# GFNet filter beside a GELU layer on one core: inverse along m2 with a stationary table, DMA transposes, new load order

## The chip, the cores and the metric

One core of a Trainium2 chip. TensorE (PE) multiplies into PSUM, VectorE (DVE), ScalarE (ACT) and GpSimd (POOL) work on SBUF (the first two also read PSUM), SyncE (SP) issues transfers. The metric is device time in microseconds (us); lower is better.

## The reference

```python
xn = layernorm(x)                      # x: 2048 tokens x 640, bf16, no scale or shift
X  = rfft2(xn); X = X * (w_r + 1j*w_i) # over tokens and width: 2048 x 321
A  = irfft2(X)                         # back to 2048 x 640
B  = gelu(xn @ w1 + b1) @ w2 + b2      # 640 -> 1536 -> 640, tanh GELU
out = x + A + B
```

## The kernel before

The 2048 tokens are 128 partitions times 16 chunks c (token 16p + c); a chunk is 128 tokens by 640.

*Planner.* Every piece of work is an `op` with candidate engines, a priority and the buffers it reads and writes. `schedule` (L201) simulates the engines with costs per operation (`mm_us`, `dve_us`, `act_us`) and takes, engine by engine, the ready op of highest priority (`PRIO`, L115); an op with two candidates goes to the engine that ends it first. SP's ops keep the written order. `sync` turns the order into semaphore waits. PSUM is eight banks, handed out by `Pool` within zones (`ZONE`, L114). So the written code gives dependences, and the planner the order on each engine.

*Stages.*
1. Loads (L494 to L530), all from SP: x in eight pieces of two chunks into XV, W1 in three pieces, the tables, the filter w in 18 pieces into Wf, and more tables.
2. Normalisation per two chunks (L543 to L559): `bn_stats` and `bn_aggr` on VectorE, a power on GpSimd, then a scale and shift (L569). The result is transposed on TensorE (L576, five 128x128 pieces) and copied to xnT. VectorE folds it twice (L588, L592; sums and differences of mirrored halves), TensorE multiplies by G (DFT over the 128 partitions, L596) and the result goes to XW.
3. Layer 1 (L606 to L618): four blocks of 512 tokens; for each of 12 feature chunks five passes of 512 columns and one GELU on ScalarE into gT.
4. Spectral stage, eight pairs (L639 to L713): a width group with table E (`five`, L621: 8 passes with 128 rows, 8 with 32 rows in quarter tiles), copied to Xb; the transform along the 16 remaining tokens with mtab in 64x64 tiles (L652), copied to Y; the filter on VectorE (L671, L676) into Z; four small copies of the remaining columns to Zs (L686 to L692); the inverse along m2 (L696): Z is the stationary operand, the 128-column table ntab the moving one, 20 passes of 128 columns a pair, so the result comes out with the width on the partitions; copied to XV (L710).
5. Width back, eight groups of two chunks with table GE (L728), copied to Wf and unfolded by VectorE (L736, L741).
6. Layer 2 per chunk (L753): 24 passes of 320 columns; two more with H (L758) add the spectral part into the same PSUM; x, loaded again (L748), has b2 added on GpSimd (L749); VectorE adds both into ost (L761), which is stored.

W2 lies in XW's space, so its load waits for all width groups of stage 4 (L716). Nearly all TensorE work has line L467 (`mms`) in the profile, nearly all copies L474 (ScalarE) or L477; they are told apart by the names of tiles.

```python
load(W2, w2v, B_w2b, F * D * 2, after=pb_ops)                       # L716
lst.append((ps(dps.slot, 128 * g, 128 * g + 128), z(r, k0, 128), rh, n == 0, n == 1))   # L705
```

Of the kernel before, what the change touches and what calls it, by code (L numbers as in the profile page):

```python
# [12 lines left out]
S = 2048  # L13
# [14 lines left out]
def _tables():  # L28

# [8 lines left out]
    for s2 in range(16):  # L38
        for m1 in range(64):
            qq, lo, pair, hi = m1 // 32, m1 // 16 % 2, m1 % 16 // 2, m1 % 2  # L40
            ang = 2 * pi * ((m1 * (16 * s1 + s2)) % 2048) / 2048
            g, h = (2 * pair + qq) * 8 + hi * 4 + lo, (2 * pair + hi) * 8 + qq * 4 + lo
# [13 lines left out]
    M = np.zeros((128, 2, 2, 2, 64))  # L56
    N = np.zeros((2, 2, 128, 128))
    for sp in range(2):
        for hi in range(2):
            for lo in range(2):  # L60
                for m2 in range(16):
                    s2 = np.arange(16)
                    a1 = 2 * pi * ((m2 * s2) % 16) / 16
                    c, s = np.cos(a1), np.sin(a1)
                    a2 = 2 * pi * ((s2 * (2 * m2 + 1)) % 32) / 32
                    c2, t2 = np.cos(a2), np.sin(a2)
                    r, u = hi * 64 + s2 * 4 + lo, hi * 64 + s2 * 4 + 2 + lo
                    p = lo * 16 + m2
                    zero = sp and hi == 0 and lo == 0
                    pq = 32 + lo * 16 + (m2 if zero else 15 - m2)  # L70
                    (rr, ir), (ri, ii) = M[:, sp, 0].transpose(1, 0, 2), M[:, sp, 1].transpose(1, 0, 2)
                    if zero:
                        rr[r, p], ri[r, p], ir[r, p], ii[r, p] = c, s, -s, c
                        rr[u, pq], ri[u, pq], ir[u, pq], ii[u, pq] = c2, t2, -t2, c2
                    else:
                        rr[r, p], rr[u, p], ir[r, p], ir[u, p] = c, s, -s, c
                        ri[r, p], ri[u, p], ii[r, p], ii[u, p] = s, -c, c, s
                        rr[r, pq], rr[u, pq], ir[r, pq], ir[u, pq] = c, s, s, -c
                        ri[r, pq], ri[u, pq], ii[r, pq], ii[u, pq] = -s, c, c, s
                    if hi:  # L80
                        continue
                    for qq in range(2):
                        r, u = s2 * 8 + qq * 4 + lo, s2 * 8 + qq * 4 + 2 + lo
                        P, Q = 64 * qq + p, 64 * qq + pq
                        NA, NB = N[sp]
                        if sp and lo == 0 and qq == 0:
                            NA[P, r], NB[P, r], NA[Q, u], NB[Q, u] = c, s, c2, t2
                            continue
                        Q = 64 * qq + 32 + lo * 16 + 15 - m2
                        NA[P, r], NA[Q, r], NB[P, r], NB[Q, r] = c, c, s, -s  # L90
                        NA[P, u], NA[Q, u], NB[P, u], NB[Q, u] = -s, -s, c, -c
    T["M"] = M
    T["N"] = np.stack([N[:, 0], N[:, 1], -N[:, 1]], axis=1).transpose(2, 0, 1, 3)
# [3 lines left out]

def mm_us(n):
    return max(n / 2400.0 + 0.003, 0.0265)
# [6 lines left out]
def act_us(n, ptr=0):  # L106
    return 0.052 + n / 1200.0 + 0.092 * ptr
# [23 lines left out]
class Pool:  # L131

# [7 lines left out]
    def find(self, buf, now):  # L140

        size, n = buf.size, len(self.free)
        lo, hi = buf.zone or (0, n)
        best = None
        for i in range(lo, hi - size + 1, size):
            if any(self.busy[i:i + size]):
                continue
            t = max(self.free[i:i + size])
            key = (max(t, now), sum(not b for b in self.busy[i & ~1:(i & ~1) + 2]), sum(not b for b in self.busy[i & ~3:(i & ~3) + 4]), t)
            if best is None or key < best[0]:  # L150
                best = (key, t, i)
        return best and best[1:]
# [18 lines left out]
BIAS = {"dve": 0.0}  # L171
LAT = {"pe": 0.2, "dve": 0.12, "act": 0.15, "pool": 0.1}


class Sched:

# [8 lines left out]
    def op(self, engs, prio, emit, reads=(), writes=(), after=(), nbytes=0, gate=(), rate=330e3, bias=BIAS):  # L185
# [4 lines left out]
        o.nbytes, o.rate, o.bias = nbytes, rate, bias  # L190
# [9 lines left out]

    def schedule(self):  # L201
        free = {e: 0.0 for e in self.engines}
        dma_free = 0.0
        pend = {e: [] for e in self.engines}
# [12 lines left out]
        def avail(o):  # L217
            o.ready = max([0.0] + [d.end for d in o.deps] + [d.start for d in o.gate])
            for e, _ in o.engs:
                pend[e].append(o)  # L220
# [4 lines left out]
        while left:  # L225
            best = None
            for e in self.engines:
                cands = []
                for o in pend[e]:
# [64 lines left out]
    def sync(self):  # L294


        allops = sorted(self.ops, key=lambda o: o.start)
        place = {o: (e, i) for e in self.engines for i, o in enumerate(self.order[e])}
        for o in self.ops:
            need = []  # L300
            for d in set(o.deps):
                if d.nbytes == 0 and d.eng == o.eng:
                    if o.eng == "pe":
                        continue
                need.append(d)
            o.waits = need

# [40 lines left out]
    def emit(self, es, last):  # L348
# [30 lines left out]
        block.tensor(run("pe"))  # L379


def bass_parallel_sum__spectral_gfnet__dense_activation_gelu__prompt_kernel(
# [21 lines left out]
    with ExitStack() as es:  # L404
# [23 lines left out]
        W1 = sb("W1", [128, 5, F])  # L428
        gT = sb("gT", [128, NFC, S])
        xnT = sb("xnT", [128, 5, S])  # L430
        XV = sb("XV", [128, 16 * D])
        XW2 = sb("XW2", [128, 16 * D])
        Wf = sb("Wf", [128, 32 * KP])
        xb4 = sb("Xb", [128, 2, 4 * KP])
        Yb = sb("Y", [128, 2, 4 * KP])
        TT = sb("T", [128, 11 * D])
        Zb = sb("Z", [128, 2, 4 * KP])
        Zs = sb("Zs", [128, 2, 2, 256])
        ost = sb("ost", [128, 3, D])
        xrt = sb("xr", [128, 4, D])  # L440
        xot = sb("xo", [128, 3, D], F32)
        PS = [es.enter_context(nc.psum_tensor(f"ps{i}", [128, 1024], F32)) for i in range(4)]

        XN, X1, XF = 0, 4 * D, 7 * D
        V = view(XV, 0, [[2048, 5], [128, 16], [1, 128]])
        Xa = view(XW2, 0, [[2048, 5], [128, 16], [1, 128]])
        W2 = view(XW2, 0, [[D, NFC], [1, D]])
        YO, Y2, YF = 0, 6 * D, 10 * D

        def ps(slot, lo, hi):  # L450
            return PS[slot // 2][:, (slot % 2) * 512 + lo:(slot % 2) * 512 + hi]

        def ps2(slot, n):
            return PS[slot // 2][:, :].rearrange("p (b n) -> p b n", b=2)[:, :, 0:n]

        psum = Pool(8)
        SMALL = [("dve", 0.066 + 128 / 960), ("pool", 0.35), ("act", act_us(128))]
        p_xn, p_x1, p_xf, p_xb, p_y, p_t, p_z, p_zs = Pool(4), Pool(3), Pool(4), Pool(2), Pool(2), Pool(2), Pool(2), Pool(2)
        p_yo, p_y2, p_yf, p_xr, p_xo, p_os = Pool(3), Pool(2), Pool(3), Pool(4), Pool(3), Pool(3)

        def load(dst, src, buf, nbytes, after=(), reads=(), rate=330e3):
            return K.op([("sp", 0.45)], 0, lambda e, _: e.dma_start(dst, src), reads=reads, writes=[buf], after=after, nbytes=nbytes, rate=rate)  # L462

        def mms(lst):
            def f(e, _):
                for o_, lw, rh, st, sp_ in lst():
                    ins = e.matmul(o_, lhsT=lw, rhs=rh, start=st, stop=sp_)  # L467
                return ins
            return f

# [9 lines left out]

        B_mh, B_xbpad, B_wpad = Buf("mhalf"), Buf("xbpad"), Buf("wpad")
# [315 lines left out]
```

## Time and profile before

| | |
|---|---|
| median of 3 runs (lowest, highest) | 176.54 us (176.17, 176.83) |
| profiled execution: span from first to last instruction (its whole time is not printed) | 175.1 us |
| TensorE busy | 154.2 us (88%) |
| VectorE / ScalarE / GpSimd busy | 109.6 / 82.1 / 32.5 us |
| moved by DMA | 16.64 MB |

Busy time is the union of an engine's instructions, and a pass's end is modelled, so a TensorE row's duration is longer than the step to the next pass. In a timeline row the first number is the start in us from the span's start, the second the time that the merged group covers, and xN the number of instructions in it. Some pass records are missing from the trace, a few per cent.

### The profile page before, as it was taken

Reading aid. Unit: us, or ns where it says so; the run is one execution under the profiler, and the core shown is the slowest. Engines: PE = TensorE matmul, PEld = TensorE weight load, DVE = VectorE, ACT = ScalarE, POOL = GpSimd, SP = SyncE. Lnnn points to the kernel's source line nnn. Section 1 sums busy time; section 2 is a strip of 40 time slices with the busy share of each in tenths; the row PEclk is TensorE's granted clock in tenths of the full one; section 3 lists DMA queues with packets and bytes.
Section 4 is the critical chain, followed back from the end, with each engine's and each line's share of the span. In section 5 each row is a group of like instructions: output and inputs, shape, how many; then the busy total and the mean of one; then the engine's idle time right before and its main releaser. Section 6 shows DMA issues by size and latency. Waiting matters only on the chain.

```text
span 175.1 us, 3375 instructions
## 1 busy us (share of the span) xinstructions
PE 154.2 (88%) x1350; PEld 95.2 (54%) x1361; DVE 109.6 (63%) x296; ACT 82.1 (47%) x129; POOL 32.5 (19%) x42
## 2 busy tenths in 40 slices
PE   0046999999999997887899999999999999998992
PEld 0034455455555454454557667777777775554771
DVE  1789959999993496999913988383745641001211
ACT  2023776668797999999875321011010104543000
POOL 1110110110110011011190033334353333000300
PEclk9999999999999999999999999999999999999999
DMA  5999999999900000005932022222232211000121
GB/s 147 304 374 384 139 103 94 100 113 102 237 16 2 4 0 4 0 4 152 373 116 75 0 79 75 75 79 75 75 113 75 78 39 37 4 0 0 37 78 40
DMA packets 14856, 16.64 MB, mean 95 GB/s; under 512 B 1272, under 2 KB 13560, under 8 KB 14840
## 3 DMA queue, kind: packets, MB, share of 16 engines
q1 hardware_dynamic: 14840, 16.42, 42.8%
q8 instruction: 11, 0.18, 0.5%
q14 instruction: 5, 0.04, 0.1%
HBM read 13.79 MB, written 2.62 MB: 94 GB/s over the span
## 4 chain that ended last, share of the span: by engine, by line
PE 77%; ACT 12%; DMA 4%; DVE 3%; issue 1%; SPq 1%
PE ps L467 74%; DMA b1t<-in_B_b_dram 4%; ACT Xb L474 3%; ACT XV L474 3%; PE ps L576 3%; ACT Y L474 3%; ACT gT L616 1%; SPq L462 1%; ACT L616 1%; DVE T L592 1%; DVE T L569 1%; ACT Zs L474 1%; DVE T L588 1%; DVE ost L761 0%; DVE stats L550 0%
## 5 line engine op out<-in xcount | busy, mean ns | idle before, releaser
L467 PE MATMUL ps<-xnT,W 128*128 128x512 bf16 x229 | 57.3, 387 | 1.9 <-ACT xnT L474 0.8
L467 PE MATMUL ps<-XW,gT 128*128 128x320 bf16 x384 | 55.4, 299 | 0.8 <-ACT gT L616 0.8
L467 PEld LDWEIGHTS ps<-XW,gT 128*128 128x128 bf16 x384 | 37.2, 98 | 16.1 <-ACT gT L616 1.9
L616 ACT ACTIVATE gT<-ps,b1col 128x512 bf16<-128x512 f32 x48 | 32.8, 686 | 19.3 <-PE ps L467 19.2
L761 DVE TENSOR_TENSOR ost<-ps,xo 128x640 bf16<-128x640 f32 x16 | 13.2, 824 | 40.4 <-PE ps L467 40.4
L467 PEld LDWEIGHTS ps<-xnT,W 128*128 128x128 bf16 x240 | 22.1, 99 | 24.3 <-ACT gT L616 2.6
L749 POOL TENSOR_TENSOR xo<-xr,b2bc 128x640 f32<-128x640 bf16 x16 | 22.4, 1405 | 53.3 <-DVE ost L761 53.1
L474 ACT ACTIVATE Wf<-ps 128x640 bf16<-128x640 f32 x8 | 5.6, 704 | 37.3 <-PE ps L467 37.3
L550 DVE BATCH_NORM_STATS2 stats<-XV 128x6 f32<-128x320 bf16 x32 | 13.9, 467 | 4.4 <-DMA XV<-in_A_x_dram 4.4
L671 DVE TENSOR_TENSOR T<-Y,Wf 128x1288 bf16<-128x1288 bf16 x16 | 12.5, 823 | 2.4 <-ACT Y L474 2.3
L554 POOL TENSOR_TENSOR rstd<-ve,mhalf 128x2 f32<-128x2 f32 x8 | 5.7, 707 | 42.9 <-DVE ve L553 42.9
L474 ACT ACTIVATE XV<-ps 128x640 bf16<-128x640 f32 x16 | 11.1, 707 | 2.5 <-PE ps L467 2.5
L467 PE MATMUL ps<-ntab,Z 128*128 128x128 bf16 x128 | 9.8, 220 | 1.8 <-ACT Y L474 1.8
L474 ACT ACTIVATE XW<-ps 128x640 bf16<-128x640 f32 x13 | 9.1, 702 | 4.7 <-PE ps L467 4.4
L592 DVE TENSOR_TENSOR T<-T 128x256 bf16<-128x256 bf16 x64 | 11.2, 233 | 0.0
L474 ACT ACTIVATE xnT<-ps 128x640 bf16<-128x640 bf16 x8 | 5.6, 701 | 11.5 <-PE ps L576 11.5
L474 ACT ACTIVATE Y<-ps 128x644 bf16<-128x644 f32 x16 | 10.9, 706 | 0.1
L477 DVE CAST Wf<-ps 128x640 bf16<-128x640 f32 x8 | 6.6, 823 | 6.8 <-PE ps L467 6.4
L736 DVE TENSOR_TENSOR Wf<-Wf 128x640 bf16<-128x640 bf16 x16 | 10.1, 673 | 0.4
L467 PEld LDWEIGHTS ps<-ntab,Z 128*128 128x128 bf16 x128 | 7.6, 98 | 4.9 <-ACT Y L474 2.6
L477 POOL COPY Zs<-Z 128x128 bf16<-128x128 bf16 x9 | 3.4, 383 | 34.5 <-DVE Z L676 34.5
L477 DVE CAST Xb<-ps 128x640 bf16<-128x640 f32 x8 | 7.1, 883 | 4.3 <-PE ps L467 4.3
(41 smaller groups left out, 139.7 us busy)
## 6 DMA issues: line engine op xcount, KB each, us to landing
XV<-in_A_x_dram SPq DMA_DIRECT2D x8, 320.0 KB, 7.9
xr<-in_A_x_dram SPq DMA_DIRECT2D x16, 160.0 KB, 2.2
out_dram<-ost SPq DMA_DIRECT2D x16, 160.0 KB, 1.8
W<-in_B_w_dram SPq DMA_DIRECT2D x3, 640.0 KB, 9.2
XW<-in_B_w_dram SPq DMA_DIRECT2D x1, 1920.0 KB, 8.4
Wf<-in_A_w_r_dram SPq DMA_DIRECT2D x7, 160.5 KB, 16.2
Wf<-in_A_w_i_dram SPq DMA_DIRECT2D x7, 160.5 KB, 15.9
gtab<-c_G SPq DMA_DIRECT2D x1, 512.0 KB, 7.4
```

The lines of the kernel that those rows point to most:

```text
L467: ins = e.matmul(o_, lhsT=lw, rhs=rh, start=st, stop=sp_)
L474: return e.activation(dst(), src(), ACT.Copy, scale=scale)
L477: return e.tensor_copy(dst(), src())
L550: K.op([("dve", 0.4)], pr, lambda e, _, c=c, h=h: e.bn_stats(stats[:, c, 6 * h:6 * h + 6], view(XV, c * D + H2 * h, [[1, H2]])), reads=[B_ ...
L554: K.op([("pool", 0.6)], pr, lambda e, _, a=a, b=b: e.tensor_tensor(out=rstd[:, a:b], in0=ve[:, a:b], in1=mhalf[:, a:b], op=ALU.pow), reads ...
L576: ins = e.transpose(ps(tps.slot, 0, 512).bitcast(BF)[:, 128 * j:128 * j + 128], xnv(128 * j, [[1, 128]]), ident[:])
L592: K.op([("dve", dve_us(2 * n, 2))], pr - 0.2, lambda e, _, op=op, x1v=x1v, xfv=xfv, o_=o_, o0=o0, o1=o1, n=n: e.tensor_tensor(out=xfv(o_, ...
L616: K.op([("act", act_us(512, 1))], pr + PRIO["gelu"], lambda e, _, q4=q4, fc=fc, hps=hps: e.activation(gT[:, fc, 512 * q4:512 * q4 + 512], ...
L671: t_ops[pair].append(K.op([("dve", dve_us(4 * KP, 2))], pr, lambda e, _, k=k, Y=Y, TB=TB, pair=pair: e.tensor_tensor(out=view(TT, TB.slot ...
L736: K.op([("dve", dve_us(D, 2))], pr + 2, lambda e, _, k=k, op=op, yo=yo, y2=y2: e.tensor_tensor(out=view(Wf, Y2 + y2.slot * 2 * D + (H2 - 1 ...
L749: K.op([("pool", pool_us(640))], 50, lambda e, _, xr=xr, xo=xo: e.tensor_tensor(out=xot[:, xo.slot, :], in0=xrt[:, xr.slot, :], in1=b2bc[: ...
L761: K.op([("dve", dve_us(640))], 95, lambda e, _, xo=xo, os_=os_, fps=fps: e.tensor_tensor(out=ost[:, os_.slot, :].rearrange("p (h n) -> p h ...
```

## The change

- *Inverse.* ntab shrinks to 64x64 tables and becomes the stationary operand; Z is the moving one, 320 columns, in four 64x64 tiles; Zs and its copies are gone. The result has its tokens on the partitions, is copied in two instructions to a buffer U (in gtab's space or behind T), and a DMA transpose per q, issued from SP, puts it into XV with the width on the partitions. The H table and the layout of the filter rows (every fourth partition) change with it.
- *x* has its own buffer X for the whole kernel and is not loaded again; XV now holds what XW held and then the transposed result. W2 has its own buffer and is loaded before the spectral stage. The final sums and stores use W1's space once layer 1 is done.
- *Loads* in order of first use: x alone for chunks 0 and 1, then in pairs; the first third of W1 from ScalarE's queue.
- *Layer 1* in blocks of 1, 1, 2, 2, 2, 4, 4 chunks. Thirty passes on a zeroed tile stand first on TensorE.
- *Width groups* of 2, 3, 3, 3, 3, 2 chunks, all full-height passes first, then the quarter-height ones. Folds take two chunks in one instruction.
- *Layer 2*: chunks 0 to 3 (`KEEP`) are done before the last stage, their sum kept in xnT's space; the 640 columns are split 512 + 128; the last chunk ends in two halves.
- *Planner*: a cost for a change of tile shape, `HOLD` to stay in a shape, other latencies and zones.

```diff
+BLOCKS = [(0, 1), (1, 1), (2, 2), (4, 2), (6, 2), (8, 4), (12, 4)]
+GROUPS = [(0, 2), (2, 3), (5, 3), (8, 3), (11, 3), (14, 2)]
+BYDMA = ()
+KEEP = (0, 1, 2, 3)
...
+        B_wps = Buf("warmps", psum)
+        pe([("128", 30 * 0.108)], 300, lambda: [(psb(B_wps.slot, [[1, 128]]), warm[:], warm[:], True, True) for _ in range(30)],
+           reads=[B_warm], writes=[B_wps])
...
+        load_x(0, 1)
+        load_w1(0, "act")
         load(ident[:], const["I"], B_id, 32768)
+        load_x(1, 1)
         load(b1t[:], b1v, B_b1, 3072)
+        load_w1(1)
+        load_x(2, 2)
+        load_w1(2)
+        load(gtab[:], const["G"], B_g, 524288)
+        for c in range(4, 16, 2):
+            load_x(c, 2)
...
+            for v in range(2):
+                dps = Buf(f"dps{pair}_{v}", psum, 2, ZONE["dps"])
+                d_ops.append(pe([("64", 2 * mm_us(H2) + 0.02)], PRIO["ipc"] - pair / 5 + 0.02 * (1 - v), lambda pair=pair, v=v, Z=Z, dps=dps: [
+                    (psb(dps.slot + qq, [[1, H2]], 0, 64 * hi, 64),
+                     part(ntab, 64 * qq, 64, (1 if pair == qq == hi == 0 else 0) * 192 + 64 * ((0, 2), (1, 0))[v][r], [[1, 64]]),
+                     part(Zb, 64 * qq, 64, Z.slot * 4 * KP + (2 * hi + r) * KP + v, [[1, 2], [2, Q4]]), r == 0, r == 1)
+                    for r in range(2) for qq in range(2) for hi in range(2)], reads=[Z, B_n], writes=[dps]))
...
+                def evac(e, name, U=U, v=v, uv=uv, dps=dps):
+                    for o_, w in ((0, 128), (512, 32)):
+                        ins = copy(lambda: uv(U, o_ + 2 * w * v, [[D, 2], [w, 2], [1, w]]), lambda: psb(dps.slot, [[512, 2], [Q4, 2], [1, w]], o_ // 4))(e, name)
+                    return ins
...
+            for qq in range(2):
+                q = 2 * pair + qq
+                K.op([("sp", 1.6)], 0, lambda e, _, q=q, qq=qq, U=U, uv=uv: e.dma_start_transpose(
+                    XV[:, :, 128 * q:128 * q + 128], uv(U, D * qq, [[1, D]])), reads=[U, B_u], writes=[B_v[q]], nbytes=163840, rate=150e3)
...
+                if kept:
+                    kps = Buf(f"kps{c}", psum, 2, ZONE["fps"])
+                    second(c, kps, 0, D, pr, [kept_ops[-2]] if len(kept_ops) > 1 else [pb_ops[-2]])
+                    xo2 = Buf(f"kx{c}")
+                    kept_ops.append(K.op([("dve", dve_us(D))], 30, lambda e, _, kps=kps, xov=xov, shaped=shaped: e.tensor_tensor(
+                        out=xov(0, D), in0=shaped(psb(kps.slot, [[1, D]])), in1=xov(0, D), op=ALU.add), reads=[kps, xo], writes=[xo2]))
```

## Rows read from the trace of the kernel before

**Rows 1.** Page, its head and part 1: busy time, share of the span, instructions.

```profile
span 175.1 us, 3375 instructions
...
PE 154.2 (88%) x1350; PEld 95.2 (54%) x1361; DVE 109.6 (63%) x296; ACT 82.1 (47%) x129; POOL 32.5 (19%) x42
```

**Rows 2.** Timeline, first 17 us: start, duration, engine, line, operation [idle before].

```profile
3.76 1.28 DVE L550 BATCH_NORM_STATS2 stats<-XV 128x6 f32<-128x320 bf16 x3 [3.76 <-DMA XV<-in_A_x_dram]
...
7.24 0.72 POOL L554 TENSOR_TENSOR rstd<-ve,mhalf 128x2 f32<-128x2 f32 x1 [6.15 <-DVE ve L553]
...
9.61 0.80 DVE L569 TENSOR_SCALAR T<-XV,rstd,nmr 128x640 bf16<-128x640 bf16 x2
...
10.11 1.25 PE L576 MATMUL ps<-ident,T 128*128 128x128 bf16 x10 [0.81 <-DVE T L569]
...
10.86 0.49 DVE L477 COPY xnT<-ps 128x640 bf16<-128x640 bf16 x1
...
15.72 0.70 ACT L474 ACTIVATE xnT<-ps 128x640 bf16<-128x640 bf16 x1 [1.04 <-PE ps L576]
...
16.48 1.46 PE L467 MATMUL ps<-xnT,W 128*128 128x512 bf16 x3 [0.80 <-ACT xnT L474]
...
19.23 1.28 ACT L616 ACT_TABLE_LOAD   x1
```

**Rows 3.** Timeline of TensorE: layer-1 passes early and later.

```profile
18.27 2.20 PE L467 MATMUL ps<-xnT,W 128*128 128x512 bf16 x5
...
24.08 1.24 PE L467 MATMUL ps<-xnT,W 128*128 128x512 bf16 x5
```

**Rows 4.** Timeline of TensorE near the end, and VectorE's last addition.

```profile
168.30 3.42 PE L467 MATMUL ps<-XW,gT 128*128 128x320 bf16 x24
...
171.56 0.43 PE L467 MATMUL ps<-Wf,htab 128*128 128x320 bf16 x2
172.03 0.82 DVE L761 TENSOR_TENSOR ost<-ps,xo 128x640 bf16<-128x640 f32 x1 [2.71 <-PE ps L467]
```

**Rows 5.** Timeline, spectral stage between the width passes.

```profile
64.47 0.73 ACT L474 ACTIVATE XV<-ps 128x640 bf16<-128x640 f32 x1
...
67.10 1.08 PE L467 MATMUL ps<-etab,XW 128*128 128x160 bf16 x16
...
68.02 0.61 PE L467 MATMUL ps<-ntab,Z 128*128 128x128 bf16 x8
...
68.58 0.61 PE L467 MATMUL ps<-ntab,Z 128*128 128x128 bf16 x8
...
74.43 1.08 PE L467 MATMUL ps<-etab,XW 128*128 128x160 bf16 x16
...
75.44 0.47 PE L467 MATMUL ps<-Xb,mtab 64*64 64x322 bf16 x8
...
75.84 0.62 PE L467 MATMUL ps<-ntab,Z 128*128 128x128 bf16 x8
...
78.13 1.08 PE L467 MATMUL ps<-etab,XW 128*128 128x160 bf16 x16
```

**Rows 6.** Windows: stretch, engines' busy time, granted clock, DMA share, GB/s.

```profile
0.00:5.00 5.00, 0.00 (x0) 0.00 (x0) 1.24 (x4) 1.28 (x1) 0.56 (x8) 1.00 0.56 158
5.00:10.00 5.00, 0.19 (x1) 0.10 (x1) 3.12 (x15) 0.00 (x0) 0.72 (x1) 1.00 1.00 334
20.00:40.00 20.00, 19.76 (x138) 10.36 (x140) 17.50 (x72) 14.63 (x23) 2.12 (x3) 1.00 1.22 101
65.00:92.00 27.00, 23.06 (x326) 14.34 (x326) 21.29 (x43) 24.37 (x44) 6.91 (x11) 1.00 0.34 105
```

**Rows 7.** Groups of instructions by form: busy, mean ns.

```profile
L616 ACT ACTIVATE gT<-ps,b1col 128x512 bf16<-128x512 f32 x48 | 32.8, 686 | 19.3 <-PE ps L467 19.2
```

**Rows 8.** Windows over the span, instructions on the tile Zs alone.

```profile
0.00:175.10 175.10, 4.40 (x32) 2.46 (x32) 2.63 (x12) 2.81 (x10) 3.90 (x10) 1.00 0.43 95
```

**Rows 9.** Timeline of SP's queue: the w_i loads.

```profile
21.95 13.31 SPq L462 DMA_DIRECT2D Wf<-in_A_w_i_dram  x9
```

More of the change, by code (lines that the diff above doesn't have):

```diff
@@ L55, in _tables @@
     T["GE"] = np.concatenate([e[:128] for e in GE] + [np.concatenate([e[128:] for e in GE])], axis=1)
-    M = np.zeros((128, 2, 2, 2, 64))
-    N = np.zeros((2, 2, 128, 128))
+    M = np.zeros((2, 64, 2, 2, 64))
+    N = np.zeros((2, 64, 3, 64))
+    s2 = np.arange(16)
     for sp in range(2):
[L59 to L91, printed above, removed]
@@ L142, in find @@
         size, n = buf.size, len(self.free)
-        lo, hi = buf.zone or (0, n)
         best = None
[L145 to L151, printed above, removed]
+        for lo, hi in buf.zone or [(0, n)]:
+            for i in range(lo, hi - size + 1, size if size != 3 else 1):
+                if any(self.busy[i:i + size]):
+                    continue
+                t = max(self.free[i:i + size])
+                key = (max(t, now), sum(not b for b in self.busy[i & ~1:(i & ~1) + 2]), sum(not b for b in self.busy[i & ~3:(i & ~3) + 4]), t)
+                if best is None or key < best[0]:
+                    best = (key, t, i)
+            if best is not None and best[1] <= now + 0.05:
+                break
         return best and best[1:]
@@ L183, in __init__, with op @@
         self.order = {e: [] for e in engines}
-    def op(self, engs, prio, emit, reads=(), writes=(), after=(), nbytes=0, gate=(), rate=330e3, bias=BIAS):
+    def op(self, engs, prio, emit, reads=(), writes=(), after=(), nbytes=0, gate=(), rate=330e3, alts=None, late=0.0):
         o = Op()
@@ L189, in op @@
         o.reads, o.writes, o.after, o.gate = list(reads), list(writes), list(after), list(gate)
-        o.nbytes, o.rate, o.bias = nbytes, rate, bias
+        o.nbytes, o.rate, o.late = nbytes, rate, late
+        o.alts, o.alt = alts, None
         o.seq = len(self.ops)
@@ L217, in avail @@
         def avail(o):
-            o.ready = max([0.0] + [d.end for d in o.deps] + [d.start for d in o.gate])
+            o.ready = max([o.late] + [d.end for d in o.deps] + [d.start for d in o.gate])
             for e, _ in o.engs:
@@ L294, in sync @@
     def sync(self):
-        allops = sorted(self.ops, key=lambda o: o.start)
         place = {o: (e, i) for e in self.engines for i, o in enumerate(self.order[e])}
         for o in self.ops:
[L300 to L306, printed above, removed]
+            o.waits = [d for d in set(o.deps) if d.nbytes or d.eng != o.eng or o.eng != "pe"]
         pos = {e: 0 for e in self.engines}
@@ L436, in bass_parallel_sum__spectral_gfnet__dense_activation_gelu__prompt_kernel @@
+        Yb = sb("Y", [128, 2 * 4 * KP])
         TT = sb("T", [128, 11 * D])
[L437 to L446, printed above, removed]
@@ L459, in bass_parallel_sum__spectral_gfnet__dense_activation_gelu__prompt_kernel @@
-        p_yo, p_y2, p_yf, p_xr, p_xo, p_os = Pool(3), Pool(2), Pool(3), Pool(4), Pool(3), Pool(3)
-        def load(dst, src, buf, nbytes, after=(), reads=(), rate=330e3):
-            return K.op([("sp", 0.45)], 0, lambda e, _: e.dma_start(dst, src), reads=reads, writes=[buf], after=after, nbytes=nbytes, rate=rate)
+        Zb = sb("Z", [128, 2 * 4 * KP])
+        PS = es.enter_context(nc.psum_tensor("ps", [128, 8 * 512], F32))
+        XN, X1, XF = 0, 4 * D, 6 * D
+        YO, Y2, YF = 0, 6 * D, 9 * D
```

541 lines of the change are left out of this document (306 added, 235 removed).

## The prediction

> **What bounds the kernel now.** I read the page's head first: TensorE is busy 154.2 of 175.1 us, VectorE 109.6, ScalarE 82.1 [rows 1]. Busy time of pipelined passes hides their pace, so I priced the passes by start-to-start times from the timeline and asked where the span exceeds that sum.
>
> *Start.* Nothing large runs before 16.48 us, when the first 512-column pass of layer 1 starts [rows 2]. The chain to it is a wait for x, the statistics, the power on GpSimd, the normalisation, transposes, and their copies for four chunks: layer 1 works on 512 tokens, so it waits for the slowest of them.
>
> *Slow passes.* Five 512-column passes took 2.20 us at 18.27 and 1.24 us at 24.08 [rows 3]: some 0.2 us more each, which is half pace, the 1.2 GHz level, after an engine that had hardly worked; the granted-clock column of the windows reads 1.00 there all the same [rows 6]. About eight passes ran so: 1.8 us.
>
> *Pace.* 24 passes of 320 columns fill 168.30 to 171.56, 0.136 us each [rows 4]. Ten of 128 columns fill 68.02 to 68.58, 0.056 each [rows 5]. That is 0.417 ns a column between them, so 160 columns are 0.069, 256 are 0.109 and 512 are 0.216. A width group (8 full and 8 quarter-height passes) goes from 67.10 to 68.02, 0.92; by columns it would be 8 x 0.069 + 2 x 0.07 = 0.69, so 0.23 goes to the two changes of tile shape. A forward group in 64x64 tiles goes from 75.44 to 75.84, 0.40, against 0.27 by columns [rows 5].
>
> *The sum before.* Layer 1, 240 x 0.216 = 51.8; layer 2 with the H passes, 416 x 0.136 = 56.6; 320 passes of 128 columns (transposes, G, inverse), 17.9; 16 width groups, 14.7; 16 forward groups, 6.4: 147.4 us. Of these 30 short ones (1.7) run before 16.48. From there to 171.99, where the last pass ends, are 155.5 us for 145.7 us of work: 9.8 are lost, 1.8 to the slow passes, 3.9 to idle time in the spectral stage (23.06 busy of 27 [rows 6]), the rest to short waits. Then come the last addition, 0.82 [rows 4], and 2.25 to the end of the span. The kernel is bound by TensorE's work behind a late start.
>
> In the spectral stage the period of one pair is 3.70 us (74.43 to 78.13 [rows 5]), with ScalarE busy 24.4 and VectorE 21.3 of 27 us [rows 6]: there the copies out of PSUM hold TensorE back.
>
> **The change part by part.** The sum is made against the profiled span, 175.1; the median, 176.54, is 1.4 above it, which I take as what lies around the span and leave.
>
> 1. *Loads and small first blocks.* Layer 1 now starts on one chunk with a third of W1. The chain: x lands at 3.76 as 320 KB together with others; as 160 KB I take 3.6 (3.0 to 3.76). Two statistics of 0.42 each, about 0.35 for mean and epsilon, the power 0.72 with about 0.25 before it and 0.2 after it for the hand-overs (my estimates; 7.24 to 9.61 holds them and a wait), 0.50 to the first transpose, 0.75 to the copy, 0.76 from copy to pass (15.72 to 16.48), less 0.16 because the chunk's copy is the faster 0.49 one [rows 2]: 7.8 us. The first W1 third is sent from ScalarE's queue beside x; 0.8 MB have moved by 5 us and 2.5 MB by 10 [rows 6], and it needs some 1.5 MB moved: 7.1 plus landing. Bounds 7.0 to 9.5; I take 7.8. The start gains 8.7, of which 1.1 was short work done before it.
>
> 2. *More, smaller layer-1 passes and GELUs.* Blocks of 1, 1, 2, 2, 2, 4, 4 chunks: 120 x 0.056 + 180 x 0.109 + 120 x 0.216 = 52.3 instead of 51.8. GELUs go from 48 to 84. At 512 columns one is 0.686 [rows 7]; a 128-column copy on ScalarE is 2.81/10 = 0.28 [rows 8]; so 24 x 0.28 + 36 x 0.42 + 24 x 0.686 = 38 us against 32.9. For the first two chunks ScalarE has 24 x 0.28, a table load of 1.28 [rows 2] and four to eight copies of 0.7, 10.8 to 13.6 us, while TensorE has 6.8 and some 3.4 of transposes and G: it is held 0.6 to 3.4 us. The last third of W1 is behind 2.65 MB, about 10.5 us, which overlaps with that. I count 3.0 lost early.
>
> 3. *Warm-up passes.* 30 idle passes on zeros before x lands; hidden by the wait for x. They should take the 1.8 us of slow passes away. If the engine falls back before 7.8 us, up to 1.8 returns, partly under the ScalarE wait.
>
> 4. *Inverse with the table stationary.* 160 passes of 128 columns (9.0 us) become 16 groups of eight 320-column passes in 64x64 tiles. The nearest row is the forward group, the same form: 16 x 0.40 = 6.4. Bounds: 4.3 without shape changes, 8.6 if each of the 16 pays two. The Zs copies go: 2.63 VectorE, 2.81 ScalarE, 3.90 GpSimd [rows 8]. Each result copy becomes two instructions: 0.73 [rows 5] becomes about 0.6 + 0.28, 16 x 0.15 = 2.4 us more. The two engines gain 3.0.
>
> 5. *Width groups of up to three.* 12 groups instead of 16: 16 x 0.69 + 12 x 0.23 = 13.8 instead of 14.7. Pairwise folds and wider final folds save instructions on VectorE; TensorE's layer-1 work hides that, nothing counted (a few us if VectorE bounds).
>
> 6. *DMA transposes.* Sixteen of 160 KB on SP's queue, each behind the copies of its pair, ahead of the stores, which are not due yet. No row shows one. Lower bound: 164 KB at 334 GB/s, 0.5 us [rows 6]. Upper: the w loads move 101 GB/s in 642-byte rows, 157 rows a us [rows 6]; 640 rows of 256 bytes at that rate are 4.1 us, and 8.2 in 128-byte pieces. I take the w loads' own spacing, 13.31/9 = 1.5 us [rows 9]. The first inverse copy starts at 64.47 [rows 5]; with the start moved by 8.7 that is 55.8. Work that needs no transposed result: all but the last width passes (6.9), the H passes (4.3) and layer 2 of ten chunks (32.6), 100.7 us, which lasts to about 7.8 + 100.7 + 7.5 = 116. So 60 us stand for 16 transposes; up to 3.75 us each they are hidden.
>  The Trainium skill (Advanced Engine Details and Errata, X-Bar Transpose) says that such transposes run as fast as ordinary transfers; by that they would be at the lower bound and the sum would be the same.
>
> 7. *x kept, W2 in its own space, four chunks kept.* The 16 reloads of x go; they were not on the path. W2 no longer waits for the width passes, so layer 2 of chunks 0 to 3 (4 x 24 passes, 13 us, one addition of 0.82 each) can fill the spectral stage. I count 4.5 lost from there on (3.9 idle and about as much in short waits before). New wait: final sums and stores use W1's space and wait for all of layer 1; behind it stand the final additions on VectorE, then the stores; TensorE has layer 2 meanwhile.
>
> 8. *Last chunk in halves.* The addition goes from 0.82 to about 0.45: 0.4 saved.
>
> Sum: TensorE's work 52.3 + 56.6 + 9.0 (160 short passes) + 13.8 + 6.4 + 6.4 = 144.5, 2.9 less. Start 7.8, work left 143.9, lost 3.0 + 4.5, end 0.45 + 2.25: span 161.9, and 1.4 around it: 163.3. I say 163.
>
> **The rivals.**
>
> *A: nothing waits.* The kept chunks need no ScalarE, so they may fill the spectral stage wholly and the early waits may be a microsecond: 163.3 - 6 = 157. For: 13 us of filler against 3.9 idle. Against: the ScalarE sum of step 2.
>
> *B: the copies bound the early and the spectral stage.* ScalarE and VectorE gain 5.1 (GELU) and 3.3 (kept sums), and lose 3.0: some 5 more over two engines, 2.7 each. Then the 2.9 saved on TensorE is worth nothing: 163.3 + 2.9 + 2.7 = 169. For: the 3.70 us period with both engines near full [rows 5, 6]. Against: 60 us of the span where both have time.
>  The Trainium skill (TensorEngine Tiling (Array Packing), PSUM Bottleneck) warns that tiles speed up TensorE but not the evacuation of PSUM; the busy shares of that stage agree, and by the rule this rival would hold.
>
> *C: the transposes bound, and it is slower.* From 3.75 us each the last width passes wait; from (60 + 13)/16 = 4.6 us each it is slower than before. At 6 us, between the two packet prices of step 6: 96 us instead of 60, 36 late: 199. For: pieces of 256 bytes or less at the w loads' rate. Against: the w loads fill 16 partitions at a time, the transposes fill all.
>
> *D: the start does not move*, because W1 from a second queue delays x: about 7 us returned, 170.
>
> **How the numbers follow.** The forecast has 0.50, A 0.22, B and D together 0.20, C 0.06, and 0.02 that it all cancels. The forecast's own range is 159 to 167. The range reaches to A and B: 154 to 172. A measurement of this kernel tells 0.5% from no change; faster by more than that: 0.91, within 0.02, slower 0.07.
>
> **What would show it.** The first layer-1 pass near 7.8 us, and 512- or 256-column passes never at half pace; ScalarE full from 8 to 20 us with TensorE waiting for it; an inverse group in 0.40; transposes under 3.75 us each with the last width groups not waiting for them; idle time of TensorE between 8 us and the end under 8 us in sum. Wrong if TensorE stands for more than 5 us ahead of the last width groups, or if the first pass comes after 10.

## The result and the profile after

The changed kernel takes 168.14 us (median of 4 runs, 167.28 to 168.47) against 176.66: ratio 0.9506, 95% interval 0.9467 to 0.9546. I had said 163, with 154 to 172 as the range; the forecast's own range, 159 to 167, ends 1.1 us below the measured time. The profiled execution took 167.86 us, with a span of 166.0.

The head of the page of the changed kernel, as in [rows 1]:

```profile
span 166.0 us, 3692 instructions
...
PE 150.2 (90%) x1520; PEld 99.4 (60%) x1539; DVE 123.8 (75%) x252; ACT 80.6 (49%) x147; POOL 30.7 (18%) x33
```

The start, from its timeline. It answers to [rows 2] and [rows 3]:

```profile
0.99 3.38 PE L469 MATMUL ps<-warm 128*128 128x128 bf16 x30 [0.99 <-DVE warm L485]
...
3.74 0.89 DVE L559 BATCH_NORM_STATS2 stats<-X 128x6 f32<-128x320 bf16 x2 [2.81 <-DMA X<-in_A_x_dram]
...
7.27 0.70 ACT L480 ACTIVATE xnT<-ps 128x640 bf16<-128x640 bf16 x1 [4.77 <-PE ps L599]
...
8.03 3.17 PE L469 MATMUL ps<-xnT,W 128*128 128x128 bf16 x28 [0.80 <-ACT xnT L480]
...
10.99 0.74 PE L599 MATMUL ps<-ident,T 128*128 128x128 bf16 x5
...
12.37 3.64 ACT L645 ACTIVATE gT<-ps,b1col 128x128 bf16<-128x128 f32 x11
```

The first layer-1 pass starts at 8.03 us, where it was 16.48. It runs at half pace, the 1.2 GHz level: 28 passes of 128 columns in 3.17 us, and five transposes in 0.74. The thirty warm-up passes also took 0.11 us each, and after them TensorE stood some 2 us, until b1 had come (6.40) and the first chunk was normalised (its transposes start at 6.52). From 12.37 to 16.01 us ScalarE does nothing but GELUs.

GELUs on ScalarE by width (busy us, then mean ns); [rows 7] had 48 of 512 columns at 686:

```profile
L645 ACT ACTIVATE gT<-ps,b1col 128x512 bf16<-128x512 f32 x24 | 16.4, 689 | 8.6 <-PE ps L469 8.5
L645 ACT ACTIVATE gT<-ps,b1col 128x256 bf16<-128x256 f32 x36 | 16.2, 477 | 2.0 <-PE ps L469 0.9
...
L645 ACT ACTIVATE gT<-ps,b1col 128x128 bf16<-128x128 f32 x24 | 7.3, 372 | 0.6 <-PE ps L469 0.3
```

Together 39.9 us, 7.1 more than before; I had estimated 38.

Two stretches of the timeline that have no counterpart before; the second holds the last transposes and the first width passes back:

```profile
45.23 3.62 POOL L781 TENSOR_TENSOR xnT<-X,b2bc 128x640 f32<-128x640 bf16 x2 [2.09 <-DMA b2bc<-in_B_b_dram]
...
46.39 3.02 DVE L612 TENSOR_TENSOR T<-T 128x512 bf16<-128x512 bf16 x4
...
49.47 0.73 PE L469 MATMUL ps<-gtab,T 128*128 128x128 bf16 x10 [1.54 <-DVE T L612]
...
50.47 2.75 POOL L781 TENSOR_TENSOR xnT<-X,b2bc 128x640 f32<-128x640 bf16 x2
...
50.98 0.91 DVE L566 SCALAR_TENSOR_TENSOR nmr<-mv,rstd 128x2 f32<-128x2 f32 x1
...
51.93 1.83 DVE L587 TENSOR_SCALAR T<-X,rstd,nmr 128x640 bf16<-128x640 bf16 x2
...
53.46 0.81 PE L599 MATMUL ps<-ident,T 128*128 128x128 bf16 x10 [1.10 <-DVE T L587]
...
65.09 0.78 PE L469 MATMUL ps<-Z,ntab 64*64 64x320 bf16 x16
...
65.69 0.73 PE L469 MATMUL ps<-Xb,mtab 64*64 64x322 bf16 x16
```

```profile
102.97 2.52 SPq L732 DMA_TRANSPOSE XV<-T  x2
...
105.20 3.40 PE L469 MATMUL ps<-xnT,W 128*128 128x512 bf16 x15
...
108.44 1.02 PE L469 MATMUL ps<-getab,XV 128*128 128x160 bf16 x16
...
108.69 4.36 POOL L781 TENSOR_TENSOR W<-X,b2bc 128x640 f32<-128x640 bf16 x3 [55.47 <-PE ps L469]
...
110.36 3.04 DVE L754 TENSOR_TENSOR Wf<-Wf 128x640 bf16<-128x640 bf16 x2
...
114.39 0.45 PE L469 MATMUL ps<-Wf,htab 128*128 128x512 bf16 x2 [1.98 <-DVE Wf L759]
```

Read the first one downwards. GpSimd adds x and b2 from 45.23 to 48.85. In that time VectorE's four folds (L612) take 3.02 us; the same four take 1.03 at 19.86, where GpSimd does nothing. The G passes wait 1.54 us for them. At 50.47 GpSimd starts again, and a two-element-wide instruction of VectorE (L566) takes 0.91 instead of 0.15: it ends at 51.89, when the first of the two additions, which took 1.40 of the 2.75, has ended (51.87). The next transposes wait 1.10. In the second stretch the unfolding (L754) takes 3.04 for two, beside 4.36 us of GpSimd; without GpSimd two take 0.89 (a kernel further down shows it), and the first final pass waits 1.98.

Two inverse groups take 0.60 us together (65.09 to 65.69), 0.30 each; a forward group took 0.40 in [rows 5]. The last two transposes are issued at 102.97 and take 1.26 us each on SP's queue; TensorE still does layer 1 until the width passes back start at 108.44, without a wait for them.

The end, as in [rows 4]: the last pass and the last addition, half as wide:

```profile
163.13 0.30 PE L469 MATMUL ps<-Wf,htab 128*128 128x320 bf16 x1
163.47 0.49 DVE L814 TENSOR_TENSOR W<-ps,W 128x320 bf16<-128x320 f32 x1 [1.27 <-PE ps L469]
```

### The profile page after: what moved, and what is told of

Same layout as the page of the kernel before. It is cut to its first block, busy times and chain, and to the rows that moved or that the text cites. A ratio compares the mean times of both kernels' runs of the same rounds, so it can differ in the third digit from the quotient of the medians.

```text
span 166.0 us, 3692 instructions
## 1 busy us (share of the span) xinstructions
PE 150.2 (90%) x1520; PEld 99.4 (60%) x1539; DVE 123.8 (75%) x252; ACT 80.6 (49%) x147; POOL 30.7 (18%) x33
## 4 chain that ended last, share of the span: by engine, by line
PE 60%; DVE 31%; issue 3%; DMA 3%; ACT 2%; SPq 1%; DVEq 0%
PE ps L469 59%; DVE stats L559 6%; DVE T L612 5%; DVE T L587 4%; DVE T L608 3%; DVE W L814 3%; DMA b1t<-in_B_b_dram 3%; DVE Wf L754 2%; DVE XV L481 2%; DVE xnT L481 2%; ACT Wf L480 1%; DVE Wf L759 1%; DVE mv L561 1%; DVE nmr L566 1%; SPq L464 1%
## 5 line engine op out<-in xcount | busy, mean ns | idle before, releaser
L469 PE MATMUL ps<-xnT,W 128*128 128x256 bf16 (+2 forms) x412 | 58.7, 296 | 2.6 <-ACT xnT L480 1.5
L469 PE MATMUL ps<-W,gT 128*128 128x512 bf16 (+2 forms) x375 | 54.8, 297 | 2.5 <-DVE W L814 1.9
L469 PEld LDWEIGHTS ps<-xnT,W 128*128 128x128 bf16 x420 | 36.6, 104 | 16.8 <-issue 2.1
L645 ACT ACTIVATE gT<-ps,b1col 128x256 bf16<-128x256 f32 (+2 forms) x84 | 39.9, 508 | 11.2 <-PE ps L469 9.8
L469 PEld LDWEIGHTS ps<-W,gT 128*128 128x128 bf16 x384 | 29.6, 98 | 24.9 <-DVE W L814 2.4
L781 POOL TENSOR_TENSOR W<-X,b2bc 128x640 f32<-128x640 bf16 x12 | 17.8, 1488 | 84.2 <-PE ps L469 55.5
L814 DVE TENSOR_TENSOR W<-ps,W 128x640 bf16<-128x640 f32 (+1 forms) x13 | 10.0, 770 | 16.6 <-PE ps L469 16.6
L559 DVE BATCH_NORM_STATS2 stats<-X 128x6 f32<-128x320 bf16 x32 | 14.5, 478 | 2.8 <-DMA X<-in_A_x_dram 2.8
L754 DVE TENSOR_TENSOR Wf<-Wf 128x960 bf16<-128x960 bf16 (+1 forms) x12 | 10.7, 924 | 0.5 <-ACT Wf L480 0.4
L759 DVE TENSOR_TENSOR Wf<-Wf 128x960 bf16<-128x960 bf16 (+1 forms) x12 | 10.2, 887 | 0.1
L612 DVE TENSOR_TENSOR T<-T 128x512 bf16<-128x512 bf16 (+1 forms) x32 | 10.2, 380 | 0.0
```

Of the source, the lines that this page charges most:

```text
L469: ins = e.matmul(o_, lhsT=lw, rhs=rh, start=st, stop=sp_, skip_group_check=True)
L559: K.op([("dve", 0.393)], pr, lambda e, _, c=c, h=h: e.bn_stats(stats[:, c, 6 * h:6 * h + 6], view(X, c * D + H2 * h, [[1, H2]])), reads=[B ...
L612: ring_ops.append(K.op([("dve", dve_us(4 * w, 2))], pr, lambda e, _, op=op, x1v=x1v, xfv=xfv, o_=o_, o0=o0, o1=o1, w=w: e.tensor_tensor(ou ...
L645: K.op([("act", act_us(128 * nt, 1))], pr + PRIO["gelu"], lambda e, _, c0=c0, nt=nt, fc=fc, hps=hps: e.activation(gT[:, fc, 128 * c0:128 * ...
L754: K.op([("dve", dve_us(320 * n, 2))], pr + 2, lambda e, _, k=k, op=op, yo=yo, y2=y2, n=n: e.tensor_tensor(out=view(Wf, Y2 + y2.slot * 3 * ...
L759: K.op([("dve", dve_us(320 * n, 2))], pr + 3, lambda e, _, k=k, op=op, y2=y2, yf=yf, n=n: e.tensor_tensor(out=view(Wf, YF + yf.slot * 3 * ...
```

## The experiments

All times are medians; ratios are to the kernel before on the same chip (its medians there: 176.40 to 176.72), and small differences are better read from them than from the times. The changed kernel stands at 168.0 us in its second measurement, which is the measure for the others.

| run | us | ratio, 95% interval |
|---|---|---|
| changed kernel again | 167.99 | 0.9500, 0.9464 to 0.9536 |
| GpSimd's additions on 8 columns | 160.17 | 0.9087, 0.9063 to 0.9111 |
| 60 warm-up passes | 166.58 | 0.9445, 0.9422 to 0.9467 |
| plain copies for transposes | 166.85 | 0.9461, 0.9437 to 0.9485 |
| kernel before + new inverse | 176.29 | 0.9974, 0.9949 to 0.9999 |
| no kept chunks | 169.15 | 0.9571, 0.9535 to 0.9606 |
| layer 1 in four blocks | 169.38 | 0.9593, 0.9560 to 0.9627 |
| b2 of chunks 0 to 6 by TensorE | 164.94 | 0.9354, 0.9318 to 0.9389 |
| the same, other additions later | 161.28 | 0.9140, 0.9111 to 0.9169 |
| the same, 60 warm-up passes | 160.73 | 0.9114, 0.9083 to 0.9144 |
| four blocks and 8 columns | 167.07 | 0.9463, 0.9431 to 0.9495 |
| kernel before, 8 columns | 176.58 | 1.0009, 0.9982 to 1.0036 |

**GpSimd's additions made short**

```diff
-  out=xov(0, D), in0=shaped(view(X, c * D, [[1, D]])), in1=shaped(b2bc[:]), op=ALU.add)
+  out=ptmp[:, 8 * c:8 * c + 8], in0=view(X, c * D, [[1, 8]]), in1=b2bc[:, 0:8], op=ALU.add)
```

> The changed kernel with the order on every engine as it was; only GpSimd's sixteen additions of x and b2 work on 8 columns instead of 640, and the sums read x itself, so b2 is left out of the output. Theory 1 (VectorE's instructions with two SBUF inputs wait while GpSimd's long additions run, at 45 to 54 us and at 108 to 126 us, and TensorE then waits for VectorE): the four 128x512 and 128x128 folds at 46.4 us take 1.0 us instead of 3.0, TensorE's idle time after 40 us falls by 4 to 6 us, 162 to 164 us in all. Rival (VectorE and ScalarE are simply full with their own copies there, the prediction's B): less than 1 us changes, 167 to 168.5.

Measured 160.17, below the 162 to 164 of theory 1: the gain is larger than it said. Windows of the changed kernel (second run) and of this one: stretch, then busy time of PE, PEld, DVE, ACT, POOL.

```profile
45.00:55.00 10.00, 7.07 (x49) 3.38 (x48) 9.12 (x18) 5.17 (x8) 5.98 (x5) 1.00 0.00 0
100.00:126.00 26.00, 22.24 (x216) 13.36 (x217) 19.60 (x26) 8.16 (x11) 5.93 (x5) 1.00 0.21 53
```

```profile
45.00:55.00 10.00, 10.00 (x81) 5.44 (x79) 7.05 (x20) 7.58 (x11) 2.28 (x5) 1.00 0.00 0
100.00:126.00 26.00, 25.03 (x243) 15.56 (x241) 19.46 (x29) 8.37 (x10) 1.45 (x6) 1.00 0.17 53
```

TensorE's busy time rises from 7.07 to 10.00 us in the first window and from 22.24 to 25.03 in the second, 5.7 us together, where the two profiled spans differ by 6.5 (164.7 and 158.2); meanwhile VectorE's falls from 9.12 to 7.05 in the first. The folds on VectorE that took 3.02 are at their plain price (as are the two normalisations that took 1.83):

```profile
45.10 1.01 DVE L613 TENSOR_TENSOR T<-T 128x512 bf16<-128x512 bf16 x4
...
48.17 0.80 DVE L588 TENSOR_SCALAR T<-X,rstd,nmr 128x640 bf16<-128x640 bf16 x2
```

The order on VectorE, ScalarE and GpSimd is the same in both kernels, and VectorE's last sums, which now read x itself, keep their 0.82 us; so the length of GpSimd's instructions makes the difference. That the prediction's rival B (the engines' own copies) was the cause is out.

**The same edit in the kernel before**

> The kernel before with GpSimd's sixteen additions on 8 columns, the sums reading the reloaded x (b2 left out), order as it was. Theory 1 (there the additions fall where VectorE has slack and TensorE has work): less than 1 us, 175.5 to 176.5. Rival (they cost that kernel as much): 168 to 172 us.

Measured 176.58 against 176.59: nothing. The collision exists there too: two unfoldings take 2.08 us at 101.34 beside an addition at 101.50, and 0.89 at 98.13. TensorE has layer 2 to do meanwhile and loses nothing.

**Layer 1 in four blocks again, with the long additions and with the short ones**

```diff
-BLOCKS = [(0, 1), (1, 1), (2, 2), (4, 2), (6, 2), (8, 4), (12, 4)]
+BLOCKS = [(0, 4), (4, 4), (8, 4), (12, 4)]
```

> The changed kernel with layer 1 in four blocks of four chunks, as before the change; loads, inverse and all else as changed. Theory 1 (the early start is worth what it moves): the first layer-1 pass comes at 14 to 16 us instead of 8.0, of which the narrow GELUs gave back a few: 172 to 175 us. Rival (ScalarE's 36 more GELUs cost as much as the start gains): 167 to 169 us.

> Layer 1 in four blocks of four chunks and GpSimd's additions on 8 columns (b2 left out), against 160.2 us with the small blocks and the short additions. Theory 1 (the early start is worth its 8 us, but with the long additions it is given back in waits on VectorE): 166.5 to 168.5 us, hardly less than the 169.4 with the long additions. Rival (the early start is worth 1.4 us in any case): 161 to 163 us.

Measured 169.38 with the long additions and 167.07 with the short ones. So the early start is worth 1.4 us in the changed kernel (168.0) and 6.9 us where nothing collides (160.17). 169.38 lies between the two expectations, 0.4 above the rival's range; the rival's reason (the GELUs) is out with 167.07, which bore theory 1 of the second run out. With four blocks the first pass comes 10.5 us later, at half pace as well, and the late window has less idle time. The window, then rows of the same run's timeline:

```profile
18.48 3.60 PE L469 MATMUL ps<-xnT,W 128*128 128x512 bf16 x8 [0.80 <-ACT xnT L480]
```

```profile
100.00:126.00 26.00, 26.00 (x226) 14.81 (x225) 17.46 (x27) 11.10 (x16) 4.11 (x3) 1.00 0.29 58
```

```profile
110.43 0.90 DVE L754 TENSOR_TENSOR Wf<-Wf 128x640 bf16<-128x640 bf16 x2
...
120.14 4.11 POOL L781 TENSOR_TENSOR W<-X,b2bc 128x640 f32<-128x640 bf16 x3 [60.97 <-PE ps L469]
```

In the window from 100 to 126 us TensorE is busy 26.00 of 26 us here and 22.24 in the changed kernel. With four blocks layer 1 lasts until 120 us, and the additions, whose results take W1's space, start only then (120.14): the first unfoldings are over, at their plain price (0.90 at 110.43), and layer-1 passes stood beside them. In the changed kernel layer 1 ends at 108.6, so the additions start at 108.69, right ahead of the first unfoldings, with no layer-1 work left. That is where the expected gain went: the start moved, and the time came back as waits for VectorE. The long additions cost 2.3 us with four blocks (169.38 to 167.07) and 7.8 with the small ones.

**60 warm-up passes**

> 60 passes on the constant tile at the start instead of 30, planned as 30, all else the same. They end at about 6 to 7.4 us, just before the first transposes. Theory 1 (ScalarE's 24 narrow GELUs hold layer 1 until 18 us whatever the pace of TensorE): the passes from 8 to 11 us come at 0.056 us, but the time changes by less than 0.7 us. Rival (the half-pace passes of 8 to 11 us are on the path): 1.5 to 2 us less, 166.3.

```profile
0.98 6.13 PE L469 MATMUL ps<-warm 128*128 128x128 bf16 x60 [0.98 <-DVE warm L485]
...
8.41 1.29 PE L469 MATMUL ps<-xnT,W 128*128 128x128 bf16 x20 [0.80 <-ACT xnT L480]
10.09 0.62 PE L469 MATMUL ps<-xnT,W 128*128 128x128 bf16 x8 [0.39 <-ACT gT L645]
```

The passes at 8.41 come at 0.056 us now, and a new wait of 0.39 for a GELU stands before the next ones. The time falls by 1.4 us by the medians and by 1.0 by the ratios, whose intervals still touch (0.9467 and 0.9464), between the two expectations. On the kernel without collisions, below, it is 0.55. So what half pace at the start costs is not told apart from nothing. The two profiled executions of the changed kernel differ there themselves: the first G passes start at 15.48 us in the first (167.86 us in all) and at 14.20 in the second (166.52); with 60 passes they start at 14.38 (166.56). The 60 passes run until 7.05 and hold the first transposes back, to 7.16 from 6.52 and 6.30. All four runs with 60 passes lie at 166.5 to 166.8, where those of the changed kernel spread from 166.5 to 168.6: the better of its executions is as fast without them.

**Plain copies for the transposes**

> The sixteen DMA transposes replaced by ordinary copies of the same 160 KB, so the inverse's result is not turned; all else the same. Theory 1 (the transposes are hidden: the last lands before TensorE has run out of layer 1 and kept layer-2 work): within 0.5 us of the changed kernel. Rival (with two U buffers the copies of the next pair but one wait for the transposes, 1.26 us of issue and some 2.6 us to landing each, and the spectral stage is paced by them): 2 us or more less.

Issues by line (us to landing at the end of a row), plain copies first, then the transposes of the changed kernel:

```profile
XV<-gtab SPq DMA_DIRECT2D x8, 160.0 KB, 2.6
XV<-T SPq DMA_DIRECT2D x8, 160.0 KB, 2.6
```

```profile
XV<-gtab SPq DMA_TRANSPOSE x8, 2.6
XV<-T SPq DMA_TRANSPOSE x8, 3.1
```

166.85 against 168.0, 1.1 us by the medians and 0.7 by the ratios, whose intervals overlap: not told apart from nothing by these runs. A transpose lands in 2.6 to 3.1 us where a plain SBUF copy of the same size takes 2.6; it holds SP's queue 1.26 us instead of 0.65 (1.29 for two). The pacing rival, 2 us or more, is out.

**The new inverse alone, in the kernel before**

Its edit is the hunk of the inverse in the diff, with the table layouts, the two U buffers and the filter rows; all else as before.

> The kernel before with one part of the change alone: the inverse with the stationary 64x64 table, its two-instruction copies into U, the DMA transposes and the table layouts that belong to it; loads, blocks, x reloads and all else as before. By the prediction's terms TensorE has 2.6 us less and the two copying engines 3.0 us less: 173.5 to 175 us. Rival (the last transposes add some 3 us of latency before the width passes back, with little filler in that kernel): 176.5 to 179 us, no gain or a loss.

176.29, ratio 0.9974: at most 0.9 us faster. The 1.5 to 3 us of the forecast's terms were not there. The rival's time came nearer, but not for its reason: no wait of TensorE for a transpose is among the waits of this run. The first reason is the price of a group that stands alone among layer-1 passes. Two such groups of this run with the five passes between them, then the same place in the kernel before:

```profile
66.46 0.48 PE L461 MATMUL ps<-Z,ntab 64*64 64x320 bf16 x8
66.88 1.25 PE L461 MATMUL ps<-xnT,W 128*128 128x512 bf16 x5
68.06 0.49 PE L461 MATMUL ps<-Z,ntab 64*64 64x320 bf16 x8
```

```profile
87.03 0.61 PE L467 MATMUL ps<-ntab,Z 128*128 128x128 bf16 x8
...
87.58 1.24 PE L467 MATMUL ps<-xnT,W 128*128 128x512 bf16 x5
88.66 0.61 PE L467 MATMUL ps<-ntab,Z 128*128 128x128 bf16 x8
```

A group and five passes take 1.60 us from start to start, where they took 1.63. The group itself went from 0.55 to 0.42 us, but the passes beside it take 1.18 us instead of 1.08. I read that as the price of the two changes of tile shape, one of which falls on the neighbours: 0.52 in all, by estimate, for 0.55. Eight of the sixteen groups stand alone like this, and TensorE's busy time falls by 0.7 us (154.2 to 153.5), not by 2.6. The other eight come in pairs, and there TensorE waits for the copies (waits in us in total, times, longest):

```profile
PE ps L461 <- ACT gtab L468: 2.0, 3, 0.9
PE ps L461 <- ACT T L468: 1.5, 4, 0.9
```

3.5 us of waits for the two-instruction copies into U stand where the kernel before has 3.6 of waits for the copies of Y and XV. So where the groups are cheaper, the copies set the pace, as the prediction's rival B said. The Trainium skill's warning on PSUM evacuation (TensorEngine Tiling (Array Packing), PSUM Bottleneck) agrees with these two rows.

**No kept chunks**

> The changed kernel with no kept chunks (KEEP empty): no layer-2 work ahead of the last stage, so four additions on VectorE fewer, all additions of x and b2 after layer 1. Theory 1 (the kept passes are what TensorE lives on while the last transposes land): TensorE stands for some 5 us before the width passes back, 171 to 174 us. Rival (layer 1 alone fills the spectral stage, and the kept chunks only move work): within 1 us of 168.

```profile
104.09 1.72 PE L469 MATMUL ps<-getab,XV 128*128 128x160 bf16 x16 [4.90 <-DMA XV<-T]
```

TensorE does stand 4.90 us for the last transposes, as theory 1 had it, but the time rises by 1.2 us only, less than theory 1's 3 and a little more than the rival's 1, with intervals that just touch. Without kept chunks there are no additions of GpSimd at 45 to 54 us either, which cost TensorE 2.6 there; the two effects together do not tell their parts apart further.

**b2 by TensorE**

```diff
+PEB = tuple(range(7))
-  e.memset(warm[:], 0.0)
+  e.memset(warm[:], 1.0 / 128)
...
-  for fc in range(f0, f0 + 3) for a, b in sums(o0, w)],
+  for fc in range(f0, f0 + 3) for a, b in sums(o0, w)] + ([
+  (psb(fps.slot, [[1, b]], a - base(o0)), warm[:], b2bc[:, a:a + b], False, False) for a, b in sums(o0, w)] if f0 == 9 and c in PEB else []),
...
+  if c not in PEB:
     K.op([("pool", 1.36)], 50, ...
```

> A whole kernel again: for chunks 0 to 6, which are the ones whose GpSimd addition falls on a busy VectorE, b2 comes from two more TensorE passes a chunk (a constant 1/128 table times b2 on all partitions) and the sums read x itself; GpSimd adds only for chunks 7 to 15. Theory 1 (shared waiting of VectorE and GpSimd): the 7.9 us that the short additions saved, less 14 passes of 0.272 for a pair of them, 1.9 us, less what chunks 7 to 15 still cost: 161.5 to 163.5 us. Rival (the short additions gained mainly because xo came free sooner for all sixteen chunks): 165 us or more.

164.94: outside theory 1's range, at the edge of its rival's. The trace shows the reason: the planner let GpSimd start the next chunks' additions as soon as layer 1 was done, right beside the first unfoldings.

```profile
106.86 4.61 POOL L783 TENSOR_TENSOR W<-X,b2bc 128x640 f32<-128x640 bf16 x3 [58.72 <-PE ps L470]
...
107.14 3.07 DVE L755 TENSOR_TENSOR Wf<-Wf 128x640 bf16<-128x640 bf16 x2
...
112.27 0.45 PE L470 MATMUL ps<-Wf,htab 128*128 128x512 bf16 x2 [2.55 <-DVE Wf L760]
```

So the additions that are left, of chunks 7 to 15, wait for the final passes of chunk 4 in the next kernel; that moves those of chunks 7 to 9:

```diff
-  reads=[B_x[c], B_b2b], writes=[xo], after=free)
+  reads=[B_x[c], B_b2b], writes=[xo], after=free + [fin_ops[4]])
```

> The whole kernel of the run before last in its kind (b2 of chunks 0 to 6 by TensorE), with the one difference that GpSimd's additions for chunks 7 to 15 wait for the final passes of chunk 4, so that they no longer start at 107 us, beside the first unfolding. Theory 1 (what was left of the loss are the three additions at 106.9 to 111.5 us, which stretched the first four unfoldings from some 3.3 to 5.0 us and let TensorE wait 2.5): 162 to 163 us. Rival (VectorE meets the later additions just as badly): 164 to 166 us.

161.28, better than I expected; the four unfoldings are at their plain price and GpSimd comes later. The rival of the run before (the short additions gained because xo came free sooner) is out as well, as chunks 7 to 15 keep their full additions here.

```profile
106.36 0.89 DVE L755 TENSOR_TENSOR Wf<-Wf 128x640 bf16<-128x640 bf16 x2
...
107.29 0.89 DVE L760 TENSOR_TENSOR Wf<-Wf 128x640 bf16<-128x640 bf16 x2
...
115.35 4.77 POOL L783 TENSOR_TENSOR W<-X,b2bc 128x640 f32<-128x640 bf16 x3 [68.00 <-PE ps L470]
```

Three additions still meet VectorE at 115 us, and TensorE waits 0.2 us for it in all. With 60 warm-up passes:

> The same with 60 passes on the constant tile at the start instead of 30. With the collisions gone, time at the start should reach the end: 1 to 1.5 us less than with 30 passes, about 161.5 us. Rival (the early stage is held by ScalarE's narrow GELUs): less than 0.5 us.

160.73 us, 0.55 less; by the intervals of the ratios (0.9111 to 0.9169 and 0.9083 to 0.9144) not told apart from the kernel above. It computes the whole reference, and beats the changed kernel by 7.3 us and the one before by 15.9. TensorE is busy 95% of its span of 159.5 us.

## Why the prediction was right, and where it was not

The direction was right, and the time lies in the stated range of 154 to 172, which had been stretched to take in rivals A and B. The forecast's own 159 to 167 missed it, and that 163 came so near was partly luck, as the fourth step shows. The sum by its steps:

- *Start*: 7.8 said, 8.03 seen (7.55 in the second profiled execution). Right, and its chain too (x at 3.74 against 3.6).
- *Around the span and the end*: 1.9 us lie around the span of the profiled execution, where I took 1.4 from the median. From the last pass, 163.43, to the end are 2.6; I said 2.7.
- *Work of TensorE*: 144.5 said. The inverse group costs 0.30 us where it stands beside another of its shape, not 0.40, as the pair at 65.09 does. That term was 1.6 too large at most (16 x 0.1). That leaves 142.9 to 144.5. Alone among 128-row passes a group costs 0.52 with what it adds to its neighbours, as the new inverse alone showed: the 0.40 of its row left out the change of shape ahead of it, which shows in the width group before (1.01 from 74.43 to 75.44, where the one at 67.10 takes 0.92 [rows 5]). GELUs cost 39.9, not 38.
- *Lost time*: the step that failed. From 8.03 to 163.43 are 155.4 us for 142.6 to 144.2 us of work (five short passes came before): 11.2 to 12.8 lost, where I counted 3.0 + 4.5. The kernel with the short additions runs from 7.64 to 155.59, 148.0 us: 3.8 to 5.4 lost. So GpSimd's additions cost 7.4 us, or 6.6 against the second profiled execution (7.55 to 162.11), whose start is like that of the short one, and all that I had named (narrow GELUs, late W1, half pace, the spectral stage) costs 3.8 to 5.4, not 7.5. The 163 came near by errors of opposite sign, and the test of under 8 us of idle time after the start was not met. I priced the additions as GpSimd's own time off the path and did not ask what they do to VectorE's instructions, although they moved: the kept ones into the normalisation, the others to the moment when layer 1 ends, where the first unfoldings wait.
- *Warm-up* (step 3): wrong. TensorE stood some 2 us after the passes, and the layer-1 passes of 8 to 11 us ran at the 1.2 GHz level (of 128 columns, where I had named those of 256 and 512). By the medians 60 passes are worth 0.55 to 1.4 us, not told apart from nothing, inside the 1.8 that I named.
- *Transposes* (step 6): 1.26 us on the queue and 2.6 to 3.1 to landing, below the 3.75 from which they would show. They started at 66.7, not 55.8; the last left the queue at 105.5, and layer 1 lasted until 108.4. That was close: without the kept chunks TensorE waits 4.9 for them. Rival C was far off.
- *Rivals*: A (157, nothing waits) is not reached even with the short additions: that kernel takes 160.2 and still loses 3.8 to 5.4. B's time (169) is close to the measured one, but for another reason: the additions, not the copies. D is out, the start moved.

The Trainium skill has the rule that I should have weighed (SBUF — State Buffer, Who interferes with whom): a VectorE instruction with two SBUF inputs contends with a GpSimd instruction that reads SBUF, for ports that only one of them holds at a time. The trace agrees: the folds, the unfoldings and L566 have two SBUF inputs. Taken one by one, the first fold ends at 47.61, after the addition that ends at 47.32, the second at 48.94, after the one that ends at 48.86, and L566 at 51.89, after 51.87. A VectorE copy out of PSUM that starts at 50.24 takes its plain 0.82 under the addition of 50.47.

Open: how much of the gain of the plain copies and of the 60 warm-up passes is real within 1 us, the parts of the two effects in the run without kept chunks, and how much of the 3.8 to 5.4 us each of the causes that I had named takes.

## What to carry to other kernels

When a start moves forward, ask whether the work behind it is still there to cover the waits that were hidden at the end: here 6.9 us of start became 1.4. Price an instruction on GpSimd also by what VectorE runs beside it, and look for pairs of rows in which one form of a VectorE instruction is twice as long in one place as in another. Price a group in another tile shape with what its two changes of shape add to the passes beside it, and ask whether copies pace the stage: here a term of 2.6 us was worth at most 0.9 when tested alone.

## What the runs showed of the hardware that was not expected

- Beside additions of 128x640 on GpSimd, VectorE's instructions with two SBUF inputs were held until an addition had ended: 0.91 us for an instruction of 0.15, and 3.02 for four that take 1.03 together. A normalisation, with one SBUF tensor and two columns of scalars, was stretched too (1.83 for two instead of 0.80). GpSimd is held too: its additions take 1.40 and 1.39 us at 50.47 and 51.83, and 2.09 at 45.23, beside two folds of VectorE (L608) that keep their 0.88.
- After thirty warm-up passes in 3.38 us and some 2 us of idle time, layer-1 passes of 128 columns from 8.03 us took 0.11 us each (1.2 GHz level); after sixty, ending at 7.1 us, those from 8.41 took 0.056 (2.4 GHz level).
- Eight 64x64 passes of 320 columns alone among 128-row passes took 0.42 us, and the five 512-column passes beside them 1.18 instead of 1.08; two such groups together take 0.60.
- A DMA transpose of 160 KB from SBUF to SBUF lands about as fast as a plain copy (2.6 to 3.1 against 2.6 us), and takes twice the time of SP's queue (1.26 against 0.65).
